# One-hot matmuls in place of a trip through DRAM for the first chunk's attention in a fused transformer block

## The chip, the cores and the metric

The kernel runs on one core of a Trainium2 chip. The metric is device time in microseconds (us) of one execution; lower is better. The five engines are named as the profile names them: PE (TensorE, the matrix engine, with its weight loads shown as PEld), DVE (VectorE), ACT (ScalarE), POOL (GpSimd) and SP (SyncE, which here only issues transfers). Each engine works through its own instructions in order, and waits at an instruction until what it needs is there.

## The reference

One block over 2048 rows of width 576, all in bfloat16: a layer norm shifted and scaled by vectors made from `c`, a local dilated attention, a second such layer norm, and a gated bilinear feed-forward layer of width 4608. Cut to what matters:

```python
W, dil = (8, 2)                     # H = 32 heads of Dh = 18
idx = pos[:, None] - (jnp.arange(W) * dil)[None, :]      # row s looks at rows s, s-2, ..., s-14
kg, vg = k[idx], v[idx]             # gathered per row and window step; idx < 0 is masked
attn = softmax(where(idx >= 0, einsum('bhsd,bhswd->bhsw', q, kg) * Dh**-0.5, -1e9))
o = einsum('bhsw,bhswd->bhsd', attn, vg)

sa, ca, ga, sb, cb, gb = split(silu(c) @ w_mod, 6)
x = x + ga * (attention(layernorm(x) * (1 + ca) + sa) @ wo)
h = layernorm(x) * (1 + cb) + sb
x = x + gb * (((h @ w_gate) * (h @ w_up)) @ w_down)
```

## The kernel before

**Tiling.** The 2048 rows are eight chunks of 256 rows (`CH`), each two halves j of 128 rows. Width 576 is four tiles of 128 and one of 64. The feed-forward layer works on groups of chunks (`GROUPS`: chunk 0 alone, then 1 and 2, 3 and 4, 5 and 6, then 7 alone): `gate_up` runs over 36 tiles of the 4608 columns, `down` over the same 36 tiles as contraction. While a group's feed-forward matmuls run, the attention of later chunks is worked off in small pieces between them; `spread` hands the pieces out by written costs. So from the first `gate_up` on, PE has matmuls nearly all the time.

**The setup stage.** Before the first `gate_up` can begin, chunk 0 must be through its attention, output projection and second layer norm, and chunks 1 and 2 through their Q, K and V projections. This stage is written out by hand, one call after another; the order of the calls is the order of the instructions on each engine. Its parts, by name:

- `load_wm`, `load_k`, `load_x`, `load_wgr`, `load_wgu` issue loads on SP, in one queue. A weight of 576 rows takes two transfers (512 rows and 64 rows). `wmA`, `wmB` and `wmC` hold blocks of `w_mod`.
- `mod_columns` makes the shift and scale columns from `wmA` or `wmB` (50 matmuls of one column); `mod_row` makes the row `ga` from `wmC`.
- `a_ln`, `a_norm` (layer norm statistics and normalisation, on DVE, the root on ACT), `a_t` (transposes on PE, evicted by ACT and DVE with shift and scale), `a_q` and `a_qj` (Q and K projections, evicted by ACT), `a_v` (V projection; its rows are evicted by ACT to `v_sb` and then written to the DRAM tensor `vd` by a POOL transfer).
- `b_ld` reads `vd` back, on POOL's queue: eight overlapping copies of 128 rows, each two rows further, into one tile `vsh` (1152 KB). So row p of the tile holds the eight value rows that query p looks at.
- `pj` (products of Q and shifted K on DVE), `lj` (sums per head by matmuls with the 0/1 matrix `ind`), `max_j` and `sum_j` (softmax on DVE, the exponential on ACT): the attention weights `attn0` of chunk 0, by query.
- `av_half` multiplies half of `vsh` by the weights on DVE (`b_mul`, 128x2304) and sums over the window with 20 matmuls by `ident` into `po`; ACT evicts to `oT`. `b_wj` is the output projection, `x1_half` the residual sum with the second norm's statistics, `transposed` the transposes into `h2T`, which `gate_up` reads.

**What sets the order around the loads.** Explicit dependencies made by `behind` hold back some transfers: the first load of `wo` waits until the first `vsh` has landed, and all loads behind it in SP's queue (the rest of `wo`, `wmC`, the residual rows) wait with it; the load of `wgr` waits for the second `vsh`; chunk 1's two `vsh` loads wait for the first two blocks `wgu`.

**The end.** `down` of the last group sums over 32 of the 36 tiles for both halves in turn, then finishes the 64-wide rests (`accr`), then the four last tiles of each half; DVE multiplies each half by `gb` (128x512), adds the residual to both halves, and SP stores each half's 128 x 576 rows.

Few lines say this best:

```python
    a_v(0, 0)                       # V, then Q and K, then the values come back through DRAM
    for g in range(3):
        a_qj(0, g, nc.scalar.copy)
    vsh_in = [b_ld(0, 0)]
...
        if dd4 == 0:
            behind(m, vsh_in[0])    # m: the first load of wo
```

Of the kernel before, what the change touches and what calls it, by code (L numbers as in the profile page):

```python
# [18 lines left out]
P = 128  # L19
# [24 lines left out]
def kernel(  # L44
# [55 lines left out]
    maskneg = consts.tile([P, W, H], BF, name="maskneg")  # L100
# [5 lines left out]
    wqk = wts.tile([P, KT, 2 * D], BF, name="wqk")  # L106
# [53 lines left out]
    def load_k(dst, wsrc, c0, n):  # L160
        r = nc.sync.dma_start(dst(slice(0, P), slice(0, KF)), wsrc[0:KF * P, c0:c0 + n].rearrange("(k p) n -> p k n", p=P))
        nc.sync.dma_start(dst(slice(0, 64), KF), wsrc[KF * P:D, c0:c0 + n])
        return r

    def load_wm(wm, bi, blk):
        return load_k(lambda p, k: wm[p, k, bi, :], w_mod, blk * D, D)
# [28 lines left out]
    zrow = sp.tile([HALO, D], BF, name="zrow")  # L195
    nc.gpsimd.memset(zrow[:], 0.0)
    nc.gpsimd.dma_start(vd[0:HALO, :], zrow[:])
    nc.gpsimd.memset(wqk[64:, KF, :], 0.0)
    for k in range(2):
# [6 lines left out]
                            pattern=[[-P, KT], [DH, H]], channel_multiplier=-1)  # L206
    nc.gpsimd.memset(maskneg[:], 0.0)
# [4 lines left out]
    for o_sb in o_sbs:  # L212
        nc.gpsimd.memset(o_sb[:, :, D:], 0.0)


    def ln_parts(src, tag):
# [15 lines left out]
        def norm(j):  # L232
            for d0, s0, n in ((0, 0, D), (D, D - 64, 64)):
                nc.vector.tensor_scalar(xn[:, j, d0:d0 + n], src(j)[:, s0:s0 + n], mv[:, j, 0:1], rstd[:, j:j + 1],
                                        ALU.subtract, ALU.mult)
        return xn, stat, rsq, norm

    def layernorm(src, tag):
# [4 lines left out]
        def norms():  # L243
            for j in range(ST):
                norm(j)
# [63 lines left out]
    def a_ln(i):  # L309
        x = x_in.pop(i)  # L310
        xn, rsq, norm = layernorm(lambda j: x[:, j, :], "a")
        aa[i] = dict(xn=xn, rsq=rsq, norm=norm)
# [54 lines left out]
    def a_v(i, j):  # L367
# [7 lines left out]
        v_sb = vstage.tile([P, DH, H], BF, name="v_sb")  # L375
# [3 lines left out]
        nc.gpsimd.dma_start(vd[r0:r0 + P, :], v_sb[:].rearrange("p d h -> p (d h)"))  # L379
# [78 lines left out]
    def av_half(j, hf, acc={}):  # L458
        b = bb[0]
        b_mul(0, j, 4 * hf, 4)  # L460
# [3 lines left out]
        v = b["vsh"][j][:].rearrange("p w d h -> p w (d h)")  # L464
        for w in range(4 * hf, 4 * hf + 4):
            for m in range(KT):
                d, m0 = (po[:, m, :], m * P) if m < KF else (po4[:], D - P)
                nc.tensor.matmul(d, lhsT=v[:, w, m0:m0 + P], rhs=ident[:], start=(w == 0 and m in (0, KF)),
                                 stop=(w == W - 1), skip_group_check=True)
# [167 lines left out]
    def down(gi, hh, bg):  # L637
        grp = GROUPS[gi]
        nj = ST * len(grp)
        last = FT - FB  # L640
        at = spread([(1.0, p) for p in bg], last)
        acc = [ps([P, 512], F32, "acc") for _ in range(nj)]
        accr = ps([P, 2 * ST, 64], F32, "accr")

        def mm_a(f, j):
            wb = wd_blk[gi * NBLK + f // FB]
            nc.tensor.matmul(acc[j][:], lhsT=hh[:, f, js(j)], rhs=wb[:, f % FB, 0:512],  # L647
                             start=(f == 0), stop=(f == FT - 1))
# [18 lines left out]
        for j in range(nj):  # L667
            for f in range(last, FT):
# [4 lines left out]
                                gb_bc[:, None, 512:D].to_broadcast([P, nj, 64]), ALU.mult)  # L673
        for j in range(nj):
            for f in range(last, FT):
                mm_a(f, j)
            nc.vector.tensor_tensor(o_ts[j][:, 0:512], acc[j][:], gb_bc[:, 0:512], ALU.mult)
# [33 lines left out]
    hT0 = aa[0]["hT"]  # L711
    nc.gpsimd.tensor_copy(sc_bc[:], sc[:, :, None].to_broadcast([P, KT, P]))
# [4 lines left out]
    a_ln(1)  # L717
    a_v(0, 0)
    for g in range(3):
        a_qj(0, g, nc.scalar.copy)  # L720
    vsh_in = [b_ld(0, 0)]
# [4 lines left out]
    def pj(j, w):  # L726
        off = HALO - DIL * (W - 1 - w) + j * P
        prods[j, w] = prodp.tile([P, KT, P], BF, name="prodj", tag="prod")
        nc.vector.tensor_tensor(prods[j, w][:], aa[0]["qT"][:, :, js(j)], aa[0]["kT"][:, :, off:off + P], ALU.mult)
# [18 lines left out]
    bb[0]["attn"] = attn0  # L748
# [11 lines left out]
    load_wm(wmB, 0, 3)  # L760
    load_wm(wmB, 1, 4)
    for dd4 in range(4):
        nk = (DH - dd4 + 3) // 4
        wsrc = bass.AP(A_wo.tensor, A_wo.offset + dd4 * D, [[DH * D, H], [4 * D, nk], [1, D]])
        m = nc.sync.dma_start(wo[dd4 * H:(dd4 + 1) * H, 0:nk, :], wsrc)
        if dd4 == 0:
            behind(m, vsh_in[0])
    load_wm(wmC, 0, 2)
    load_res(0)

    for w in range(2):
        pj(0, w)
    a_norm(1)
    for w in range(2, 4):
        pj(0, w)
    a_v(0, 1)
    vsh_in.append(b_ld(0, 1))
    for g in range(3):
        a_qj(1, g, nc.scalar.copy)
    for w in range(4):  # L780
        lj(0, w)
        pj(0, w + 4)
    a_t(1, False)
    for w in range(4, 8):
        lj(0, w)
    for w in range(2):
        pj(1, w)
    max_j(0)
    for w in range(2, 4):
        pj(1, w)  # L790
    a_q(1, 0)
# [3 lines left out]
    for w in range(4, 6):  # L795
        pj(1, w)
    sum_j(0)
    for w in range(6, 8):
        pj(1, w)
    a_q(1, 1)  # L800
    for w in range(4, 8):
        lj(1, w)
    max_j(1)
    a_q(1, 2)
    a_q(1, 3)
    av_half(0, 0)
    sum_j(1)
    a_q(1, 4)
    av_half(0, 1)
    a_v(1, 0)  # L810
    a_v(1, 1)
    mod_row(lambda p, k: wmC[p, k, 0, :], ga_bc)
    av_half(1, 0)
    x1_half = b_wj(0)
    a_ln(2)
    aa[2]["rsq"]()
    av_half(1, 1)
    aa[2]["norm"]()
# [110 lines left out]
```

## Time and profile before

| | us |
|---|---|
| median of 3 runs (lowest, highest) | 574.32 (572.67, 574.69) |
| the profiled execution, its time | 576.45 |
| its span, first to last instruction | 574.4 |
| its setup stage, until the first `gate_up` matmul (L595) starts | 62.36 |
| PE busy in the span | 548.4 |

The span is what the profile's views show; the profiled execution's own time is 2.05 us longer, and 2.13 us above the median of the runs. Matmuls of a stage overlap one another, so a row "x20, 1.29" of PE is 20 matmuls started one after another in about 1.1 us, with the last one's way through the array behind it. A number in square brackets at a timeline row is the idle time of that engine before it, with what ended it. In a list of waits the columns are total us, how many, and the longest. The chain of work that ended last is followed back from the last instruction, so its rows are what set the time.

### The profile page before, as it was taken

How to read it: one execution, taken by the hardware profiler on the slowest of the kernel's cores; microseconds unless marked ns; L12 is line 12 of the kernel's file. 1: busy time of each engine (PE TensorE's matmuls, PEld its weight loads, DVE VectorE, ACT ScalarE, POOL GpSimd, SP SyncE). 2: the span in 40 equal slices, each digit the busy share in tenths (PEclk: the TensorE clock that was granted, in tenths of full speed). 3: DMA queues.
4: the chain of work that ended last, by engine and by line, in shares of the span. 5: the costliest groups of instructions: out<-in, count | busy, mean ns of one | idle time of the engine just before them, and what ended most of it. 6: DMA issues, size and time to landing. Idle time of an engine off the chain costs nothing.

```text
span 574.4 us, 14284 instructions
## 1 busy us (share of the span) xinstructions
PE 548.4 (95%) x6024; PEld 320.3 (56%) x6058; DVE 323.7 (56%) x743; ACT 236.8 (41%) x546; POOL 66.0 (11%) x101
## 2 busy tenths in 40 slices
PE   3969998999999999999999999999999999999996
PEld 2846787666544444556444444555444444558863
DVE  5657679697568767613559759331647521324211
ACT  2533564434355555133145555113255552006630
POOL 5110201121300000111300000111200101110010
PEclk9997999999999999999999999999999999999999
DMA  8779999658756943648855924549854775468820
GB/s 248 241 220 279 354 299 328 194 156 264 247 179 217 289 126 69 123 133 191 292 194 184 296 96 120 106 114 280 296 167 138 231 213 184 124 188 241 283 72 34
DMA packets 90415, 115.05 MB, mean 200 GB/s; under 512 B 22288, under 2 KB 79712, under 8 KB 90224
## 3 DMA queue, kind: packets, MB, share of 16 engines
q1 hardware_dynamic: 77936, 65.69, 39.9%
q0 software_dynamic: 11808, 48.46, 26.4%
q8 instruction: 47, 0.77, 0.6%
q14 instruction: 16, 0.13, 0.1%
q10 hardware_dynamic: 608, 0.00, 0.1%
HBM read 105.14 MB, written 4.74 MB: 191 GB/s over the span
## 4 chain that ended last, share of the span: by engine, by line
PE 85%; DVE 6%; DMA 6%; ACT 1%; issue 1%; SPq 1%; DVEq 0%; ACTq 0%; POOLq 0%
PE pg L595 25%; PE pu L595 20%; PE acc L647 20%; PE pq L349 5%; PE accr L652 4%; PE lg L403 3%; PE pv L372 3%; PE pw L498 2%; DMA wmC<-in_w_mod_dram 2%; DMA vsh<-vd 1%; DMA wv<-in_A_wqkv_dram 1%; DMA vd<-v_sb 1%; DVE vsh L431 1%; DVE hh L624 1%; PE pa L298 1%
## 5 line engine op out<-in xcount | busy, mean ns | idle before, releaser
L595 PE MATMUL pg<-h2T,wgu 64*128 64x512 bf16 (+1 forms) x1440 | 276.1, 333 | 0.0
L595 PE MATMUL pu<-h2T,wgu 64*128 64x512 bf16 (+1 forms) x1440 | 272.4, 333 | 0.9 <-DMA wgu<-in_B_w_up_dram 0.9
L595 PEld LDWEIGHTS <-wgu 64*128 64x128 bf16 x2880 | 143.6, 94 | 107.6 <-DMA wgu<-in_B_w_up_dram 1.3
L619 ACT CAST u_sb<-pu 128x512 bf16<-128x512 f32 (+1 forms) x180 | 90.2, 501 | 160.9 <-PE pg L595 147.1
L647 PE MATMUL acc<-wd,hh 128*128 128x512 bf16 x516 | 135.1, 380 | 0.1
L624 DVE TENSOR_TENSOR hh<-g_sb,u_sb 128x512 bf16<-128x512 bf16 (+1 forms) x180 | 66.5, 370 | 106.0 <-ACT g_sb L620 101.4
L652 PE MATMUL accr<-wd,hh 128*128 128x64 bf16 x544 | 94.5, 193 | 1.4
L647 PEld LDWEIGHTS <-hh 128*128 128x128 bf16 x576 | 56.0, 98 | 64.2 <-issue 1.7
L620 ACT CAST g_sb<-pg 128x512 bf16<-128x512 f32 (+1 forms) x180 | 91.2, 506 | 0.1
L158 POOL DMA_DIRECT2D wd<-in_B_w_down_dram x41 | 31.0, 757 | 290.5 <-PE accr L652 247.4
L595 PE MATMUL pu<-h2T,wgr 64*128 64x512 bf16 (+1 forms) x180 | 60.3, 335 | 0.6 <-DVE dd L412 0.6
L595 PE MATMUL pg<-h2T,wgr 64*128 64x512 bf16 (+1 forms) x180 | 60.3, 335 | 0.0
L652 PEld LDWEIGHTS <-hh 128*128 128x128 bf16 x576 | 52.4, 98 | 2.2
L431 DVE TENSOR_TENSOR vsh<-vsh,attn 128x1152 bf16<-128x1152 bf16 (+1 forms) x60 | 45.8, 790 | 5.3 <-DMA vsh<-vd 5.3
L349 PE MATMUL pq<-hT,wqk 128*128 128x256 bf16 (+1 forms) x405 | 45.9, 262 | 1.0 <-ACT hT L252 0.4
L393 DVE TENSOR_TENSOR prod<-qT,kT 128x1280 bf16<-128x1280 bf16 x56 | 44.4, 819 | 0.0
L349 PEld LDWEIGHTS <-wqk 128*128 128x128 bf16 x405 | 34.4, 99 | 8.0 <-issue 1.9
L595 PEld LDWEIGHTS <-wgr 64*128 64x128 bf16 x360 | 21.1, 94 | 14.6 <-issue 1.3
L387 POOL DMA_DIRECT2D vsh<-vd x16 | 14.3, 895 | 113.8 <-DVE o_sb L442 68.2
L352 ACT CAST qT<-pq 128x512 bf16<-128x512 f32 x16 | 9.3, 584 | 42.9 <-PE pq L349 42.9
L672 DVE TENSOR_TENSOR t_r<-accr,gb_bc 128x256 bf16<-128x256 f32 (+1 forms) x5 | 1.9, 372 | 39.4 <-PE accr L652 39.4
L403 PEld LDWEIGHTS <-prod 128*128 128x128 bf16 x560 | 16.0, 96 | 12.0 <-DVE prod L393 6.3
(131 smaller groups left out, 435.2 us busy)
## 6 DMA issues: line engine op xcount, KB each, us to landing
wd<-in_B_w_down_dram POOLq DMA_DIRECT2D x41, 576.0 KB, 4.8
wgu<-in_B_w_gate_dram SPq DMA_DIRECT2D x45, 512.0 KB, 4.5
wgu<-in_B_w_up_dram SPq DMA_DIRECT2D x45, 512.0 KB, 6.0
vsh<-vd POOLq DMA_DIRECT2D x16, 1152.0 KB, 9.1
vd<-v_sb POOLq DMA_DIRECT2D x16, 144.0 KB, 5.1
x_r<-in_A_x_dram SPq DMA_DIRECT2D x8, 288.0 KB, 9.7
out_dram<-o_t SPq DMA_DIRECT2D x16, 144.0 KB, 7.0
vsh<-in_B_w_down_dram POOLq DMA_DIRECT2D x4, 576.0 KB, 5.1
```

The source lines that it names most:

```text
L158: return nc.gpsimd.dma_start(wb[:], B_w_down[r0:r0 + FB * P, :].rearrange("(k p) n -> p k n", p=P))
L349: nc.tensor.matmul(pq[:, gi, :], lhsT=wqk[:, kt, m * P:(m + 1) * P], rhs=hT[:, kt, cols], start=(kt == 0), stop=(kt == KT - 1))
L372: nc.tensor.matmul(pv[:], lhsT=hT[:, kt, js(j)], rhs=wv[:, kt, 0:VA * DH], start=(kt == 0), stop=(kt == KT - 1))
L393: nc.vector.tensor_tensor(prod[:], aa[i]["qT"][:], aa[i]["kT"][:, :, off:off + CH], ALU.mult)
L403: nc.tensor.matmul(b["lg"][:, j, w, :], lhsT=prod[:, m, js(j)], rhs=ind[:, m, :], start=(m == 0), stop=(m == KT - 1))
L431: nc.vector.tensor_tensor(v, v, at, ALU.mult)
L595: return nc.tensor.matmul(bank[:, 0:N], lhsT=lhs, rhs=rhs, start=first, stop=last, skip_group_check=True)
L619: nc.scalar.copy(u[:, 0:N], pu[:, 0:N])
L620: nc.scalar.copy(g[:, 0:N], pg[:, 0:N])
L624: nc.vector.tensor_tensor(hh[:, f, 0:N], gu[0][:, 0:N], gu[1][:, 0:N], ALU.mult)
L647: nc.tensor.matmul(acc[j][:], lhsT=hh[:, f, js(j)], rhs=wb[:, f % FB, 0:512], start=(f == 0), stop=(f == FT - 1))
L652: nc.tensor.matmul(accr[:, j, :], lhsT=hh[:, f, js(j)], rhs=wb[:, f % FB, 512:D], start=(f == 0 and j == 0), stop=(f == FT - 1), skip_grou ...
```

## The change

It touches the setup stage's chunk 0 and the last group's end.

1. **Values stay, weights move.** Chunk 0's V rows are kept in SBUF (`v0`), by key; of them only the last 16 rows are written to `vd`, for chunk 1. The attention weights, which are by query, are shifted to the keys: `shift_attn` runs 8 matmuls of 32 columns per half with slices of the one-hot matrix `shf`, and ACT copies the result to `at_k`. `av_mul` multiplies the V rows by these weights (DVE, 128x2304, both operands broadcast), and `av_sum` moves the products back to the queries while it sums: its 20 matmuls per quarter use slices of `shf` where `ident` stood. For the second half the 16 rows above it are made apart: `halo_values` (two matmuls), `halo_attn` (8 matmuls), one DVE product and 5 more matmuls in `av_sum`. The one-hot matrices are made on POOL: four memsets and twelve selects. The two `vsh` loads of chunk 0, the writes of its other 240 rows to `vd`, and the zero rows of `vd` go.
2. **Loads in one row.** `wmA` and `wmB` come as blocks of 1152 columns in one transfer each (and one for the last 64 rows). `wqk` is loaded as Q (576) and K (576) in place of three pieces; POOL copies K's last 64 columns next to Q's last 64.
3. **Order.** Q and K are loaded and projected ahead of V; the eight products of a half stand together; the layer norms of chunks 1 and 2 are normalised on ACT (four activations of 576 and 64 columns) and not on DVE.
4. **No holding back.** The loads of `wo`, `wgr` and chunk 1's `vsh` no longer wait for others by `behind`.
5. **The end.** In the last group the last eight tiles are left to the end in place of four; the second half's 512 columns are summed as two banks of 256, each multiplied, added and stored as soon as it is done; the 64-wide rests are done first.

The diff, cut to its core:

```diff
-    load_wm(wmA, 0, 0)
-    load_wm(wmA, 1, 1)
+    load_wm(wmA, 0)
+    load_k(lambda p, k: wqk[p, k, 0:D], A_wqkv, 0, D)
+    load_k(lambda p, k: wqk[p, k, DP:DP + D], A_wqkv, D, D)
     load_x(1)
     load_k(lambda p, k: wv[p, k, :], A_wqkv, 2 * D, D)
-    load_k(lambda p, k: wqk[p, k, 0:D], A_wqkv, 0, D)
-    load_k(lambda p, k: wqk[p, k, D:DP], A_wqkv, 2 * D - 64, 64)
-    load_k(lambda p, k: wqk[p, k, DP:2 * D], A_wqkv, D, D - 64)
...
+    shf = sp.tile([P, P + 2 * HALO], BF, name="shf")
+    p_q = sp.tile([P, (W - 1) * HALO + P], BF, name="p_q")
+    p_v = sp.tile([P, W, HALO], BF, name="p_v")
+    p_o = sp.tile([P, HALO], BF, name="p_o")
+    for t in (shf, p_q, p_v, p_o):
+        nc.gpsimd.memset(t[:], 0.0)
+    ones_at(shf[:], HALO, [[-1, P + 2 * HALO]], 1)
...
+    for w in range(W):
+        ones_at(p_o[:], -HALO * w, [[-1, HALO]], 1)
...
+        def norm_act():
+            nm = sp.tile([P, ST], F32, name="ln_nm", tag="ln_nm", bufs=2)
+            nc.vector.scalar_tensor_tensor(nm[:], mv[:, :, 0], -1.0, rstd[:], op0=ALU.mult, op1=ALU.mult)
+            for j in range(ST):
+                for d0, s0, n in ((0, 0, D), (D, D - 64, 64)):
+                    nc.scalar.activation(xn[:, j, d0:d0 + n], src(j)[:, s0:s0 + n], ACTF.Identity, bias=nm[:, j:j + 1],
+                                         scale=rstd[:, j:j + 1])
...
+        p0 = 0 if i else P - HALO if j else P
+        if p0 < P:
+            nc.gpsimd.dma_start(vd[r0 + p0:r0 + P, :], v_sb[p0:P].rearrange("p d h -> p (d h)"))
...
+    def shift_attn(j, attn, at_k):
+        r = ps([P, W, H], F32, "rot")
+        for w in range(W):
+            d = HALO + DIL * (W - 1 - w)
+            nc.tensor.matmul(r[:, w, :], lhsT=shf[:, d:d + P], rhs=attn[:, j, w, :], start=(w == 0), stop=(w == W - 1),
+                             skip_group_check=True)
+        nc.scalar.copy(at_k[:], r[:])
...
+    def av_mul(j, hf, v, at_k):
...
+        nc.vector.tensor_tensor(b["vsh"][j][:, ws], v[:, None, :, :].to_broadcast([P, 4, DH, H]),
+                                at_k[:, ws, None, :].to_broadcast([P, 4, DH, H]), ALU.mult)
...
+    nc.gpsimd.tensor_copy(wqk[:, :, D:DP], wqk[:, :, 2 * D:2 * D + 64])
...
-        if dd4 == 0:
-            behind(m, vsh_in[0])
...
+    for g in range(3):
+        a_qj(0, g, nc.scalar.copy)
+    a_ln(1)
+    for w in range(W):
         pj(0, w)
+    aa[1]["rsq"]()
     for g in range(3):
         a_qj(1, g, nc.scalar.copy)
+    aa[1]["norm"]()
+    v0[0] = a_v(0, 0)
+    for w in range(W):
+        lj(0, w)
+    max_j(0)
+    v0[1] = a_v(0, 1)
+    a_t(1, False)
     for w in range(4):
         pj(1, w)
     mod_columns(wmB, 1)
     for w in range(4):
         lj(1, w)
+    sum_j(0)
+    for w in range(4, W):
         pj(1, w)
+    a_q(1, 0)
+    shift_attn(0, attn0, at_k[0])
+    hv = halo_values(v0[0])
+    for w in range(4, W):
+        lj(1, w)
+    av_mul(0, 0, v0[0], at_k[0])
     a_q(1, 1)
     max_j(1)
     a_q(1, 2)
+    av_mul(0, 1, v0[0], at_k[0])
     a_q(1, 3)
+    av_sum(0, 0)
     sum_j(1)
     a_q(1, 4)
+    av_sum(0, 1)
+    shift_attn(1, attn0, at_k[1])
+    ha = halo_attn(attn0)
     a_ln(2)
     aa[2]["rsq"]()
+    a_v(1, 0)
+    av_mul(1, 0, v0[1], at_k[1])
+    mod_row(lambda p, k: wmC[p, k, 0, :], ga_bc)
     aa[2]["norm"]()
+    x1_half = b_wj(0)
...
+    av_mul(1, 1, v0[1], at_k[1])
+    av_sum(1, 0, hv)
...
+    a_v(1, 1)
...
+    av_sum(1, 1)
     a_t(2, False)
     x1_half = b_wj(1)
     load_x(3)
-    behind(load_wgr(), vsh_in[1])
+    load_wgr()
...
-    behind(b_ld(1, 0), wgu_in[0])
-    behind(b_ld(1, 1), wgu_in[1])
+    b_ld(1, 0)
+    b_ld(1, 1)
...
-        last = FT - FB
+        last = FT - (2 * FB if gi == NG - 1 else FB)
+        halves = [((0, 512),)] * (nj - 1) + [((0, 256), (256, 512)) if gi == NG - 1 else ((0, 512),)]
...
+                for h, (c0, c1) in enumerate(halves[j]):
+                    for f in range(last, FT):
+                        mm_a(f, j, (h,))
+                    cs = slice(c0, c1)
+                    nc.vector.tensor_tensor(o_ts[j][:, cs], acc[j][h][:], gb_bc[:, cs], ALU.mult)
+                    nc.vector.tensor_tensor(o_ts[j][:, cs], o_ts[j][:, cs], xs[j][:, cs], ALU.add)
+                    c1 = D if c1 == 512 else c1
+                    nc.sync.dma_start(out_flat[r0:r0 + P, c0:c1], o_ts[j][:, c0:c1])
```

More of the change, by code (lines that the diff above doesn't have):

```diff
@@ L463, in av_half, with add @@
         po, po4 = acc[j]
[L464 removed]
+        v = bb[0]["vsh"][j][:].rearrange("p w d h -> p w (d h)")
+        def add(src, m, c, first, last, rhs):
+            d, m0 = (po[:, m, c], m * P) if m < KF else (po4[:, c], D - P)
+            nc.tensor.matmul(d, lhsT=src[:, m0:m0 + P], rhs=rhs, start=first, stop=last, skip_group_check=True)
         for w in range(4 * hf, 4 * hf + 4):
+            d = HALO - DIL * (W - 1 - w)
             for m in range(KT):
[L467 to L469 removed]
+                add(v[:, w], m, slice(0, P), w == 0 and m in (0, KF), w == W - 1, shf[:, d:d + P])
+            if w == 0 and halo is not None:
+                for m in range(KT):
+                    add(halo[:].rearrange("p d h -> p (d h)"), m, slice(0, HALO), False, False, p_o[:])
         if hf == 1:
@@ L759 @@
     load_x(2)
-    load_wm(wmB, 0, 3)
-    load_wm(wmB, 1, 4)
+    load_wm(wmB, 3)
     for dd4 in range(4):
```

135 lines of the change are left out of this document (70 added, 65 removed).

## The prediction

> **What bounds the kernel now.** I read the chain first, cut to the setup stage (start, length, what).
>
> ```profile
> 4.67 7.80 DMA wv<-in_A_wqkv_dram
> 12.51 2.27 PE pv L372 x5
> ...
> 15.81 6.21 DMA vd<-v_sb
> ...
> 22.58 8.61 DMA vsh<-vd
> ...
> 33.03 10.16 DMA wmC<-in_w_mod_dram
> ...
> 43.33 0.59 PE pa L298
> ...
> 46.22 2.25 PE po L468 x20
> ```
>
> Up to 43.3 us the chain is transfers: V is loaded, projected, written to DRAM and read back, and only then does SP go on to `wo` and `wmC`. The waits of SP, PE and DVE in this stage say who pays:
>
> ```profile
> SPq L765 <- DMA vsh<-vd: 14.8, 1, 14.8
> ```
> ```profile
> PE pa L298 <- DMA wmC<-in_w_mod_dram: 3.5, 1, 3.5
> ```
> ```profile
> 41.28 1.36 DVE L431 TENSOR_TENSOR vsh<-vsh,attn 128x2304 bf16<-128x2304 bf16 x1 [5.28 <-DMA vsh<-vd]
> ```
>
> SP stood 14.8 us, so `wmC` came late and PE stood 3.5 us; DVE stood 5.3 us for the second `vsh`. The stages (us, each engine's busy time and count, PEclk, DMA share, GB/s) show what the PE gap costs beyond itself:
>
> ```profile
> 22.00:32.00 10.00, 8.31 (x174) 7.33 (x172) 8.90 (x24) 3.54 (x7) 1.57 (x3) 1.00 0.42 136
> ```
> ```profile
> 40.00:43.30 3.30, 0.00 (x0) 0.01 (x1) 2.02 (x3) 0.37 (x2) 0.55 (x2) 0.95 1.15 313
> 43.30:49.70 6.40, 6.16 (x35) 3.90 (x37) 3.58 (x10) 1.10 (x4) 0.00 (x0) 0.50 1.01 236
> 62.40:107.00 44.60, 42.00 (x809) 35.30 (x808) 33.28 (x72) 23.98 (x74) 5.40 (x8) 1.00 0.96 315
> ```
>
> The DMA engines are 42% busy while SP is held (22 to 32 us). After the gap PE gets a clock of 0.50 for 6.4 us, so about 3.2 us are lost on top of 3.5. From 62.4 us PE is busy 42.0 of 44.6 us, and so on to the end: what the setup stage gains is kept unless a load falls behind. The end itself is a chain on DVE:
>
> ```profile
> 568.25 1.74 PE acc L647 x8
> ...
> 570.02 0.69 DVE o_t L677
> 570.71 0.33 DVE o_t L680
> ...
> 571.14 0.34 DVE o_t L680
> ```
>
> **The change: front.** I follow the new order engine by engine and sum to the start of the first `gate_up` matmul, now 62.36. `wmA`: its second half let PE go at 9.54; one transfer of the same bytes ahead of everything else but x, I take 9.3 (8.5 if longer rows help, 10.3 if PE must wait for the tail). Behind it, 10 to 16 us moved 299 GB/s and 15 to 20 us 323: 0.66 MB each 2.1 us, so Q 11.4, K 13.5, x of chunk 1 14.4, V 16.4, `wmB` 21.5, `wo` 23.6, `wmC` 26; all 1 us earlier to 3 us later at the ends. 50 `mod_columns` matmuls at 0.92/25: 1.8, to 11.1; columns and first evictions, 10.50 to 12.1 before: 1.6, to 12.7. Before, PE was at half rate from 12.5 to about 15.9 (a 504-column matmul 0.41 us, later 0.21), so Q and K of half 0 start at 0.104 us each: 25 take 2.6, to 15.3; the last 20 are half at the slow rate, 1.6, to 16.9. K's 64 copied columns: POOL's added memsets and selects are 4 of 0.2 to 0.3, 4 of 0.29 to 0.47 and 8 of 16 columns, under the 0.29 of 128 columns, at most 5.4 us in all; the zero rows that go took 1.5. POOL had reached 8.2, so it is free by 12.1 and the copy (half the 0.72 of `sc_bc`) ends at 13.5+0.45=14.0, before PE wants it at 14.8: nothing, covered by the Q matmuls; 1 us if the copy took twice as long and K were 0.5 late. ACT evicts K (0.59, and 0.2 behind PE) at 17.7; before, the first `pj` ran at 19.11.
>
> **Middle.** DVE: eight `pj` at 0.445 end at 21.3 (before 25.6, with other work between). PE meanwhile: 45 Q/K matmuls 2.7, `a_v` 1.23, the mask and 40 `lj` 1.33, to 22.2; then `a_v` 1.23, transposes 0.57, `mod_columns` 1.6, to 25.6. ACT's normalisation, 2 of 576 and 2 of 64 columns: the nearest rows are 0.59 (128x512) and 0.21 (128x64), so 1.7 us where DVE took 1.18; it ends at 23.3, just as PE comes to the transposes (23.4): nothing, but each 0.1 us more shows. From here DVE leads: `max_j` 0.85, evictions 0.7, four `pj` 1.8, columns 0.5, `sum_j` 1.4, to 28.5; four `pj`, to 30.3; then `av_mul` 1.35 by L431's row, `max_j` 0.85, `av_mul` 1.35, `sum_j` 1.4, to 35.3. PE waits some 2.1 us in all in this piece (1.9 before in 22 to 34 us), then runs through: `a_q` 2.7, `av_sum` 1.13, `a_q` 1.09, `av_sum` 1.13 to 36.6, where before the second half's `vsh` was still to come. New on PE: `shift_attn` twice and `halo_attn`, 24 matmuls at the 0.030 of `lj`, 0.75; `halo_values` 0.26; 5 halo matmuls 0.15: 1.2 us. On ACT: 0.37 twice, 0.8, 0.2; ACT is busy under half of this stage, and `at_k` of half 1 comes at 38.0, DVE's products at 39.4 and 41.4, PE wants them at 40.8 and 43.3.
>
> **Back.** `a_v` 1.23, `mod_row` 1.24 at full rate (2.9 before), `b_wj` 1.21, `av_sum` 1.28, `a_v` 1.23, `av_sum` 1.13, to 44.4; transposes 0.57; 0.6 for `oT`'s eviction; `b_wj` 1.21; Q and K of chunk 2, transposes and V as before: 55.0. These sums leave out small gaps: the same steps of before, from 50.2 to 62.4, took 12.15 us where my way of summing gives about 11.8, so I add 1.0 over the stage. 56.0, that is 6.4 us off; 8.2 at the good end, 3 at the bad. It agrees with what goes: gap and half rate 6.7, front 1.4, less 1.2 of new matmuls.
>
> Loads that I cost at nothing: `wgr` and three `wgu` (4.3 MB) follow x of chunk 3, whose buffer is free at 23.3; at 300 GB/s they land by about 44, 12 us ahead. Chunk 1's `vsh` loads now wait for its V rows only (`a_v` at 38 and 43): landed by 60, wanted some 18 us after the first `gate_up`, at 74. Behind them POOL's queue holds loads wanted at 100. If that cover goes, `gate_up` starts late one for one.
>
> **First group and end.** In the first `gate_up` PE waited 0.9 us for `wgu`, PEld 1.2; 2.3 MB of `vsh` now lie further ahead: 0.4 off (0 to 2.1). At the end, behind the last matmul, 0.69+0.33+0.44+0.10 become 128x256 steps: 0.43 (between 0.69 for 512 and 0.29 for 128) and 0.28 (between 0.42 and 0.18): 0.85 off; the last store has no other beside it, 0.2; 16 matmuls of 256 for 8 of 512 cost nothing (0.109 against 0.215). 1.0 off (0.6 to 1.4).
>
> Sum: 6.4+0.4+1.0 = 7.8. The profiled execution took 576.45 (span 574.4), 2.13 above the median 574.32; the median becomes 566.5.
>
> **A rule against it.** The row: PE's half rate lasted 3.4 us after 12.5 but 6.4 us after 43.3. The Trainium skill (TensorE: Matmul & The Clock Gate, Part 1) says that the activity window is free-running, so the release shifts with where the first matmul falls. By the rows I used 3.4; by the rule the front could get the 6.4 of the other start, 3 us more at half rate, 1.5 us: 568.0. The trace agrees that two starts can differ; I leave it inside the forecast's bounds.
>
> **The rivals.**
> - DVE's product at one element a cycle because now both operands are broadcast (before: one). 128x256 and 128x512 from PSUM take 0.42 and 0.69, 1.06 ns per element, so 2304 take 2.6 and not 1.35. Four of them on DVE's leading piece: 1.6 to 2.5 us on the path after the slack of 1.4 to 1.9. 568.8. Against it: L431's broadcast is at full pace already.
> - Loads late: one order in SP's queue, and everything behind Q and K moves with them. K at 17 and `wmB` at 24 give 3.2 us: 569.7. For it: loads of 64 KB and up took 7 to 10 us to land; against it: there is less to load.
> - The start is given back: the DMA engines were 0.96 busy from 62.4 to 107, so an earlier `gate_up` only waits for its weights. 573.3, the end's gain alone. Against it: PE waited only 2.1 us for them, and 2.6 MB less is moved.
> - Slower: PE's waits for DVE between 24 and 31 us bring the clock down as the gap at 40 did. Each us of matmul work at half rate costs one; half rate from 26 to about 47, some 18 us of matmul work at the full rate, less 7.8, gives 584. It decides from 7.8+2.9=10.7 us of such work. Against it: 22 to 32 us had PE 83% busy with waits of up to 1.4 and a clock of 1.00.
>
> **How the numbers follow.** About 0.5%, 2.9 us, is what a measurement of this kernel can tell from no change: faster is below 571.4. Chances: forecast 0.64, broadcast 0.10, late loads 0.14, given back 0.07, clock 0.05. The forecast's own bounds (3+0+0.6 to 8.2+2.1+1.4 off) are 562.6 to 570.7; taking in the broadcast and the late loads, 563 to 571 leaves out about 2 in 10. Faster: 0.64+0.10 and most of 0.14, 0.85; same 0.09; slower 0.06.
>
> **What would show it.** Right: the first L595 matmul near 56; no DVE wait for `vsh` and no PE wait over 2 us after 13 us; clock 1.00 from 17 us on; `wmC` landed before 30; the first 128x2304 product near 31 at 1.35 us; the last DVE step 0.75 us after the last matmul. Wrong: a mean near 2.6 at `av_mul`; PE waiting for `wqk`, `wmB` or `wgu`; a clock of 0.5 past 20 us; the first `gate_up` longer than the 44.7 us that it took.

## The result, and the profile after

The changed kernel takes 568.55 us (median of 5 runs, 567.49 to 570.20) where the kernel before takes 574.32 (5 runs, 572.67 to 574.79): 5.8 us less, a ratio of 0.9911 with a 95% interval of 0.9886 to 0.9937. Forecast were 566.5 and a range of 563 to 571. The sign and the range held; 2.0 of the 7.8 us did not come.

Every profile below is one execution. The changed kernel's has a span of 568.4 us (its own time is 570.20, 1.65 above the median; that of before was 2.13 above its own), against 574.4. The chain of work that ended last, in order of time, cut to the setup stage (start, length, what):

```profile
4.80 9.11 DMA wqk<-in_A_wqkv_dram
14.05 0.46 POOL wqk L801
14.55 5.38 PE pq L375 x70
...
30.43 4.73 PE pq L375 x25
...
35.15 1.12 PE po L534 x20
...
```

Where the chain of before ran through `vd` and `vsh`, this one runs through K's load, POOL's copy and then almost only PE. The longest waits by engine and line in 8 to 58 us (us in total, times, longest) say the same:

```profile
DVE vsh L523 <- ACT at_k L494: 2.9, 1, 2.9
POOL wqk L801 <- DMA wqk<-in_A_wqkv_dram: 2.8, 1, 2.8
...
PE pm L311 <- DMA wmA<-in_w_mod_dram: 1.1, 1, 1.1
...
PE pq L375 <- DVE hT L276: 1.0, 1, 1.0
```

No wait for `wmC` or for a `vsh` load is left, and PE's two waits of 1 us lie ahead of Q. DVE's wait of 2.9 us at half 1's `av_mul` holds nobody up. The new product takes 1.35 us, as the one of before did (1.36), and ACT's normalisation is longer than I took (2.29 for 1.7); first the instructions of the product's line (duration in ns, min/median/max), then two rows of the timeline (start, length):

```profile
L523 DVE TENSOR_TENSOR vsh<-v,at_k x4: 1349/1352/1358, 30.0 to 41.5; 128x2304 bf16<-128x2304 bf16 x4
```
```profile
21.48 2.29 ACT L257 ACTIVATE ln_xn<-x_t,ln_nm,ln_rstda 128x576 bf16<-128x576 bf16 x4 [0.92 <-DVE ln_nm L254]
...
29.97 1.35 DVE L523 TENSOR_TENSOR vsh<-v,at_k 128x2304 bf16<-128x2304 bf16 x1
```

The stages (us, each engine's busy time and count in the order PE, PEld, DVE, ACT, POOL; then PEclk, DMA share, GB/s):

```profile
22.00:27.50 5.50, 5.28 (x109) 4.23 (x106) 4.09 (x12) 4.62 (x12) 0.66 (x1) 1.00 1.10 267
27.50:34.40 6.90, 6.49 (x55) 4.45 (x53) 6.70 (x13) 3.29 (x9) 0.00 (x0) 0.51 1.03 214
34.40:56.80 22.40, 22.11 (x254) 17.30 (x255) 15.53 (x40) 15.57 (x43) 3.25 (x5) 1.00 0.90 281
56.80:101.40 44.60, 42.02 (x809) 35.26 (x808) 33.26 (x72) 23.99 (x74) 5.39 (x8) 1.00 0.85 275
```

PE is busy 22.11 of 22.40 us up to the first `gate_up`, and that takes the same 44.6 us as before: nothing of the earlier start is given back there. But from 27.5 to 34.4 us the granted clock is 0.51 although PE waits for nothing long: the 25 `pq` matmuls of the chain take 4.73 us there, and 2.7 where the same step runs at full rate (50.28 us, 2.73). DVE's part of the end is as forecast; its last step ends 0.79 us behind the last matmul (1.60 before):

```profile
564.39 0.37 DVE o_t L758
564.76 0.02 issue
564.78 0.29 DVE o_t L759
```

Difference of the two spans, 6.0 us: the start of the first `gate_up` matmul 5.6 (62.36 to 56.77), from there to the last matmul 0.1, from that to the end of the span 0.3 (4.42 to 4.12).

### The profile page after: what moved, and what is told of

Read it like the earlier page. It is cut to its first block, busy times and chain, and to the rows that moved or that the text cites. A ratio compares the mean times of both kernels' runs of the same rounds, so it can differ in the third digit from the quotient of the medians.

```text
span 568.4 us, 14437 instructions
## 1 busy us (share of the span) xinstructions
PE 549.2 (97%) x6090; PEld 325.8 (57%) x6125; DVE 322.6 (57%) x740; ACT 242.0 (43%) x559; POOL 66.7 (12%) x113
## 4 chain that ended last, share of the span: by engine, by line
PE 89%; DVE 7%; DMA 2%; ACT 1%; issue 1%; SPq 1%; POOL 0%; ACTq 0%; POOLq 0%
PE pg L668 26%; PE pu L668 20%; PE acc L723 20%; PE pq L375 7%; PE accr L727 4%; PE pv L398 3%; PE lg L432 3%; PE pw L571 2%; DMA wqk<-in_A_wqkv_dram 2%; DVE vsh L460 1%; PE po L534 1%; DVE hh L697 1%; DVE prodj L816 1%; DVE prod L422 1%; DVE vsh L467 0%
## 5 line engine op out<-in xcount | busy, mean ns | idle before, releaser
L668 PEld LDWEIGHTS <-wgu 64*128 64x128 bf16 x2880 | 141.5, 94 | 107.4 <-DMA wgu<-in_B_w_up_dram 1.0
L723 PE MATMUL acc<-wd,hh 128*128 128x512 bf16 (+1 forms) x534 | 134.4, 372 | 0.2
L375 PE MATMUL pq<-hT,wqk 128*128 128x256 bf16 (+1 forms) x405 | 49.7, 279 | 1.8 <-DVE hT L276 1.3
L375 PEld LDWEIGHTS <-wqk 128*128 128x128 bf16 x405 | 37.5, 106 | 9.5 <-issue 1.3
L460 DVE TENSOR_TENSOR vsh<-vsh,attn 128x1152 bf16<-128x1152 bf16 x56 | 40.4, 751 | 0.0
L668 PEld LDWEIGHTS <-wgr 64*128 64x128 bf16 x360 | 19.0, 94 | 14.6 <-issue 1.3
L416 POOL DMA_DIRECT2D vsh<-vd x14 | 12.5, 892 | 84.9 <-DVE o_sb L471 68.8
```

The costliest lines, as they stand in the source:

```text
L375: nc.tensor.matmul(pq[:, gi, :], lhsT=wqk[:, kt, m * P:(m + 1) * P], rhs=hT[:, kt, cols], start=(kt == 0), stop=(kt == KT - 1))
L460: nc.vector.tensor_tensor(v, v, at, ALU.mult)
L668: return nc.tensor.matmul(bank[:, 0:N], lhsT=lhs, rhs=rhs, start=first, stop=last, skip_group_check=True)
L723: nc.tensor.matmul(a[:], lhsT=hh[:, f, js(j)], rhs=wb[:, f % FB, c0:c1], start=(f == 0), stop=(f == FT - 1))
```

## The experiments

Two questions were open. First, the clock of 0.51: it is the place of the rival that I had given 0.05, so does it fall because of what runs there, and what does it cost? Second, of what is the gain made: of the gap at 40 us and the clock behind it, as I summed it, of the order of the loads, of the end, or of the trip as such? My theory throughout was the sum in the prediction.

**Does work on PE between 22 and 27 us hold the clock?** Between 23.3 and 26.7 us PE runs transposes, 50 matmuls of one column and 20 of 32, with no wait over 0.34 us. Two kernels add matmuls whose result nobody uses behind `mod_columns(wmB, 1)`, with equal time and very different numbers of columns:

```diff
+    fill = ps([P, 512], F32, "fill")
+    for _ in range(6):
+        nc.tensor.matmul(fill[:], lhsT=ident[:], rhs=wv[:, 0, 0:512], start=True, stop=True)
```

> The changed kernel with six more matmuls of 512 columns on PE (their result is used by nobody) behind the second mod_columns, where the changed kernel's trace has 3.4 us of transposes, 1-column and 32-column matmuls in a row (23.3 to 26.7 us) before the clock falls to 0.50 (27.6 to 34.4 us). Theory A, the clock is granted by how many columns PE streams, so those 3.4 us look idle to it: the clock stays 1.00 to the first gate_up, which starts at 54.5 to 55.5 in place of 56.8; about 566.7 us, 1 to 2 us faster than the changed kernel though PE has 1.3 us more work. Theory B, the clock fell because of PE's short waits for DVE: the fall stays, gate_up starts 1 us later at 57.8, about 569.5 us.

The other has 42 matmuls of 32 columns (`fill[:, 0:32]`, `wv[:, 0, 0:32]`) in that place:

> The same place and nearly the same added PE time (42 matmuls of 32 columns at 0.030 us, 1.3 us), but few columns. Theory A (columns): the clock falls as in the changed kernel or earlier, gate_up starts at 57.5 to 58.5, about 569.5 to 570 us. Theory C, the clock is granted by the time in which PE has any matmul under way: it stays 1.00 as with the dense filler, gate_up at 55, about 566.7 us. Theory B (waits): falls too, 569.5 us.

Measured: 568.91 us (ratio 0.9929, 0.9907 to 0.9950) and 568.55 (0.9929, 0.9907 to 0.9951), no different from the change; the 1 to 2 us of theory A did not come. The stage of the clock's fall, in the profile of the first and then of the second:

```profile
27.50:34.40 6.90, 6.61 (x90) 5.64 (x88) 6.76 (x14) 3.86 (x10) 0.00 (x0) 1.00 1.04 209
```
```profile
27.50:34.40 6.90, 6.36 (x87) 5.38 (x86) 6.73 (x13) 3.95 (x10) 0.00 (x0) 1.00 1.03 207
```

Both held the clock, so columns alone are not what counts. In all the traces of this study that have the change's setup stage with K at its place and no filler there, six, the clock fell behind the thin stretch, for 3.4 us in five and 6.8 in one; in the two with a filler it did not. Over all runs the mean clock of the whole execution, in which falls at other places count too, was 0.999 or more in 6 of 12 with filler and in 3 of 17 runs of the change (plain, again, and with the old end). But the filler costs its own 1.2 to 1.3 us, and a fall of 3.4 us at half rate costs 1.7: it buys nothing that can be measured. What decides the fall, whether the spacing, the columns or the moment, is not settled.

**The end taken back.** The changed kernel with the last `down` as it was:

```diff
-        last = FT - (2 * FB if gi == NG - 1 else FB)
+        last = FT - FB
-        halves = [((0, 512),)] * (nj - 1) + [((0, 256), (256, 512)) if gi == NG - 1 else ((0, 512),)]
+        halves = [((0, 512),)] * nj
-        if gi == NG - 1:
+        if False:
```

> The changed kernel with the end of the kernel before (four tiles left, both halves as whole banks of 512, both residual sums behind the last matmul). By the prediction's term the end is worth 1.0 us: 569.5 us. By the two traces, in which last matmul to end of span is 4.4 us before and 4.1 after, it is worth 0.3: about 568.9 us; the span then ends about 2.8 us behind DVE's last step, where the changed kernel has 3.3.

569.60 us (ratio 0.9942, 0.9920 to 0.9963). The change itself was timed on another chip: by the medians this is 1.05 us above it, by the ratios 1.8, and the intervals overlap. Beside the kernel before, on one chip, what is left without the new end is 3.3 us (2.1 to 4.6). The same setup code had one fall of 3.4 us here, not two, and started the first `gate_up` at 54.80 instead of 56.77: the two windows of the first trace are not a constant of the kernel.

**The hold taken from SP's queue in the kernel before.** The trip stays; `wo` and `wmC` no longer wait for it:

```diff
         m = nc.sync.dma_start(wo[dd4 * H:(dd4 + 1) * H, 0:nk, :], wsrc)
-        if dd4 == 0:
-            behind(m, vsh_in[0])
```

> The kernel before without the one dependency that holds the loads of wo (and with it wmC and all behind it) until the first vsh has landed; everything else as before. Theory D, the trip through DRAM is the cost: wmC is there before PE wants it, but vsh now shares the DMA engines, DVE still waits 5 us or more for the second vsh and PE's clock still falls; 0 to 2.5 us faster than before, 572 to 574.3 us. Theory E, the held queue is the cost: PE's wait of 3.5 us and the half clock go, 5 us or more faster, 569.3 us or less.

574.77 us, 1.0031 of before (1.0005 to 1.0057): slightly slower, so theory E fell, and the 0 to 2.5 us that theory D allowed did not come either. PE no longer waits for `wmC`, the clock falls for 3.4 us from 49.9 instead of for 6.8 from 43, the first `gate_up` comes at 58.89, and yet nothing is gained over the runs. The chain of the setup (start, length, what):

```profile
22.54 10.22 DMA vd<-v_sb
...
33.04 5.97 DMA vsh<-vd
...
39.10 1.36 DVE vsh L431
...
49.43 3.60 PE pq L349 x18
```

The second `vsh` lands at 39.0; DVE's product, two layer norms and ACT's evictions hang on it, and PE comes to `a_q(2, 0)` behind them. The queue's wait was one way in which the trip was paid, not the only one.

**The end alone, on the kernel before** (its whole `down` is that of the change, nothing else is):

```diff
-        last = FT - FB
+        last = FT - (2 * FB if gi == NG - 1 else FB)
...
+        if gi == NG - 1:
+            for j in range(nj):
+                nc.vector.tensor_tensor(o_ts[j][:, 512:D], t_r[:, j, :], xs[j][:, 512:D], ALU.add)
...
```

> The kernel before with only the new end (the last down stage of the change, nothing else). Theory of the prediction: the end is worth 1.0 us, so the time is 1.0 us under the kernel before on this chip, ratio 0.9983; last DVE step 0.75 us behind the last matmul. Rival, from the two traces: last matmul to end of span went from 4.4 to 4.1 us only, since what follows the last DVE step grew from 2.8 to 3.3 us, so 0.3 us, ratio 0.9995. The kernel of the change with the old end gave 569.6 against 568.55 for the whole change, on two chips, which speaks for 1.0.

572.75 us against 574.14 beside it, ratio 0.9972 (0.9953 to 0.9990): 1.4 us by the medians, 0.6 to 2.7 by the interval. The 0.3 of the pair of traces is ruled out, barely. What the pair hid lies in what follows the last DVE step until the span ends. With the old end it is 2.8 us in the kernel before and 3.7 in the changed one; with the new end it is 2.5 here and 3.3 in the change. So the new end shortens the time from the last matmul to the end of the span by 1.1 us in either kernel (4.42 to 3.30, 5.27 to 4.12), and the rest of the change lengthens it by 0.8. The last store takes 1.6 us to land here and in the change; behind its landing the closing steps of the program take 0.9 us here and 1.7 in the change. Why they do was not tried.

This execution told more about the setup, which is word for word that of before. `wmC` was there in time, the clock stayed at 1.00, and still the first `gate_up` matmul came only at 58.23. Its stages where before had the gap and the half rate, and then its chain:

```profile
40.00:43.30 3.30, 3.12 (x36) 2.12 (x34) 3.13 (x8) 0.96 (x4) 0.55 (x1) 1.00 1.01 225
43.30:49.70 6.40, 4.16 (x48) 3.12 (x46) 6.16 (x18) 2.64 (x8) 0.00 (x0) 1.00 1.04 294
```
```profile
22.49 7.49 DMA vd<-v_sb
29.98 0.28 issue
30.26 9.75 DMA vsh<-vd
40.11 1.36 DVE vsh L431
...
48.91 1.49 ACT hT L252 x3
50.43 2.13 PE pq L349 x18
```

Gap and half rate are not in every execution of before. Where they are missing, DVE's chain behind the trip takes their place: from 43.3 to 49.7 us DVE is busy 6.16 of 6.40 and PE 4.16.

**The gap of before filled.** 14 matmuls with an unused result, where PE had stood for `wmC`:

```diff
     a_v(1, 1)
+    fill = ps([P, 512], F32, "fill")
+    for _ in range(14):
+        nc.tensor.matmul(fill[:], lhsT=ident[:], rhs=wv[:, 0, 0:512], start=True, stop=True)
     mod_row(lambda p, k: wmC[p, k, 0, :], ga_bc)
```

> The kernel before with 14 matmuls of 512 columns whose result nobody uses, put between a_v(1, 1) and mod_row, where PE stood 3.5 us for wmC. They fill the gap (14 by 0.22 = 3.0 us) and take nothing from any engine that is waited for. Theory of the prediction (the gap brings PE to a clock of 0.50 for 6.4 to 6.8 us, of which half is lost): the clock holds at 1.00 from 43 to 50 us, the first gate_up matmul starts near 59.1 instead of 62.4, and the time is 3.2 us under the kernel before, ratio 0.9944. Rival A: the clock falls all the same, now or a window later, by a rule that goes not by this gap alone: no gain, ratio 1.000. Rival B: the stage is bound by DVE's wait for the values and not by PE: the clock holds and the start moves by less than 1 us.

573.81 us against 574.14, ratio 1.0003 (0.9983 to 1.0024): no gain; the 3.2 us of my theory did not come, though the clock held as it said. In its profile the clock holds through the filler and behind it:

```profile
39.00:42.30 3.30, 3.30 (x21) 1.55 (x20) 2.73 (x6) 0.70 (x2) 1.00 (x2) 1.00 1.21 331
42.30:50.00 7.70, 7.30 (x81) 5.42 (x80) 6.78 (x19) 3.37 (x11) 0.00 (x0) 1.00 0.99 258
```

The first `gate_up` matmul comes at 58.40: 4.0 us before the 62.36 of the first trace, but level with the 58.23 of the kernel just told, which has neither gap nor filler. So a held clock is worth what I said against the execution that I priced from, and nothing against one that does not lose it.

**Warming PE ahead of Q.** In all traces so far the first `pq` matmuls are slow, at a listed clock of 1.00: they start 0.107 us apart, and later 0.056. Half microseconds in which this changes; the number in brackets counts the `pq` matmuls under way, some of which began just before; in the filler kernel with 512 columns and in that with 32, whose code is the same up to there:

```profile
15.00:15.50 0.50, 0.50 (x9) 1.00 1.10 316
15.50:16.00 0.50, 0.50 (x12) 1.00 1.07 263
```
```profile
17.50:18.00 0.50, 0.50 (x9) 1.00 1.10 406
18.00:18.50 0.50, 0.50 (x13) 1.00 1.05 392
```

The step to the fast spacing comes at 15.4 in one and at 17.8 in the other, and the projections end 1.05 us apart. The experiment:

```diff
+    warm = sp.tile([P, 512], BF, name="warm")
+    nc.vector.memset(warm[:], 0.0)
+    fill = ps([P, 512], F32, "fill")
+    def warm_up(n):
+        for _ in range(n):
+            nc.tensor.matmul(fill[:], lhsT=warm[:, 0:P], rhs=warm[:], start=True, stop=True)
+    warm_up(10)
...
+    warm_up(2)
     mod_columns(wmA, 0)
+    warm_up(3)
```

> The kernel of the change with 15 matmuls of 512 columns whose result nobody uses ahead of Q: 10 at the very start, 2 behind the first transposes, 3 behind mod_columns(wmA). In four traces of the same front PE's first matmuls of Q and K took 0.065 us each and more until 15.3, 16.8, 17.1 and 17.9 us and 0.038 behind that, at a listed clock of 1.00. Theory: PE needs some microseconds of work, counted from a point that differs between executions, before it runs at full rate; with work from 1.5 us on it is at full rate before Q begins. Then the 70 matmuls behind K's arrival take 4.2 us instead of 4.4 to 5.7, the first gate_up matmul starts 1.0 us earlier, and the time is 1.0 us under the change on the same chip, with less scatter. Rival: the slow rate is that of the loads of Q and K or of the first use of the weights: no change.

569.07 us (ratio 0.9905, 0.9883 to 0.9928), no different from the change on that chip. The warming worked and was lost again, as the granted clock of these stages shows:

```profile
6.00:11.60 5.60, 3.84 (x65) 2.37 (x64) 2.30 (x13) 0.94 (x4) 4.59 (x20) 1.00 1.07 292
11.60:15.00 3.40, 2.94 (x24) 2.37 (x24) 1.67 (x7) 1.44 (x4) 0.86 (x2) 0.52 1.09 320
```

PE was at full rate by 6.9 (two 512-column matmuls in 0.59 us, where ten took 4.06 at the start), and fell for exactly 3.4 us just as Q began; Q's first 20 matmuls took the same 2.58 us as without warming.

**The changed kernel again**, on that chip:

> The changed kernel again, on the chip of the other three, as their measure. Expected 0.991 of the kernel before; and the clock in its profiled execution between 24 and 36 us, which fell for two stretches of 3.4 us in one execution and for one in another with the same code: theory (the fall depends on where the chip's own window lies over the thin matmuls from 23.3 to 26.7 us): none, one or two such stretches. Rival (PE's waits decide): two, as in the first.

569.31 us, ratio 0.9913 (0.9891 to 0.9934): the gain repeats on a second chip. In the setup the clock fell once, from 25.6 to 29.0 us, and the first `gate_up` matmul came at 53.88; my theory would have allowed none, one or two, so this says little for it. The clock fell a second time in the first `gate_up`, from 87.1 to 90.5 us, and from the first `gate_up` matmul to the last matmul this execution took 509.4 us where the first took 507.5.

**V and x(1) loaded ahead of Q and K, in the changed kernel:**

```diff
     load_wm(wmA, 0)
-    load_k(lambda p, k: wqk[p, k, 0:D], A_wqkv, 0, D)
-    load_k(lambda p, k: wqk[p, k, DP:DP + D], A_wqkv, D, D)
     load_x(1)
     load_k(lambda p, k: wv[p, k, :], A_wqkv, 2 * D, D)
+    load_k(lambda p, k: wqk[p, k, 0:D], A_wqkv, 0, D)
+    load_k(lambda p, k: wqk[p, k, DP:DP + D], A_wqkv, D, D)
```

> The changed kernel with the loads of x(1) and V ahead of those of Q and K, the order that before had; nothing else is moved. Theory: the front is set by K's arrival. K comes 0.96 MB later, at some 300 GB/s 3.2 us, so POOL's copy ends near 17.6 instead of 14.5; PE is warm by then, and the 70 matmuls take 3.9 us instead of 4.4 to 5.7, so they end near 21.6 instead of 18.9 to 20.0. The first gate_up matmul is 1.6 to 2.7 us later and the time some 2 us above the changed kernel: about 0.995 of the kernel before instead of 0.991. Rival (PE has slack behind the projections, as DVE's products and not PE set the stage; or x being early makes up for it): no difference from 0.991.

571.63 us, ratio 0.9931 (0.9912 to 0.9950). By the ratios 1.1 us above the change, by the medians (on different chips) 2.3 to 3.1: near the 2 expected, though the two intervals overlap. PE's waits:

```profile
PE pq L375 <- DMA wqk<-in_A_wqkv_dram: 3.5, 1, 3.5
...
PE pq L375 <- POOL wqk L801: 0.8, 1, 0.8
```

K's matmuls began at 18.07, half a microsecond behind the forecast, but PE was not at full rate: the 70 took 6.09 us instead of 3.9, and the first `gate_up` came at 58.86, 2.1 us behind the change's first trace and 5.0 behind its second. So the slow start is not over at a fixed time of the kernel: with PE idle from 11.4 to 14.9 us the full rate came at 22.3.

**The order alone, in the kernel before** (Q and K ahead of x and V in the loads, and their projections of half 0 ahead of the first values; the trip stays):

```diff
-    load_x(1)
-    load_k(lambda p, k: wv[p, k, :], A_wqkv, 2 * D, D)
     load_k(lambda p, k: wqk[p, k, 0:D], A_wqkv, 0, D)
...
+    load_x(1)
+    load_k(lambda p, k: wv[p, k, :], A_wqkv, 2 * D, D)
...
-    a_ln(1)
-    a_v(0, 0)
     for g in range(3):
         a_qj(0, g, nc.scalar.copy)
+    a_ln(1)
+    a_v(0, 0)
```

> The kernel before, with one part of the change alone: Q and K loaded ahead of x(1) and V, and the projections of Q and K of half 0 ahead of the first values on PE; the values still go through DRAM. Theory: the trip through DRAM sets the stage, V arrives some 4 us later (16.4 instead of 12.5), so everything that waits for the shifted values is later by 2 to 4 us and the kernel 1.5 to 4 us slower than before, ratio 1.003 to 1.007: the order of the loads pays only once the trip is gone. Rival: the order itself is what gained, by PE starting on Q while V loads: faster than before by 1 us or more.

575.58 us against 575.01, ratio 1.0011 (0.9993 to 1.0029): neither what I expected nor a gain. V's first projection ran 4.3 us later (16.76 for 12.51), but the second half's, which the chain goes through, stayed where it was (18.17 for 18.29), and so did the first `gate_up` (58.63). It is the second half's trip that counts; the order has no value while it is there.

This trace tells something else: PE stood for `wmC` here too, and no half rate came behind it (a wait; then a stage):

```profile
PE pa L298 <- DMA wmC<-in_w_mod_dram: 2.6, 1, 2.6
```
```profile
43.30:49.70 6.40, 6.19 (x76) 5.05 (x77) 6.17 (x17) 2.83 (x9) 0.00 (x0) 1.00 1.00 235
```

With the gap and without the half rate the first `gate_up` starts 0.4 us behind the 58.23 of the kernel that has neither. So far as these single traces show it, the gap by itself is nearly free, and what made the first trace late is the half rate behind it.

**Chunk 1's normalisation back on DVE, in the changed kernel:**

```diff
-        xn, rsq, norm = layernorm(lambda j: x[:, j, :], "a", i < 3)
+        xn, rsq, norm = layernorm(lambda j: x[:, j, :], "a", i == 2)
```

> The changed kernel with the normalisation of chunk 1 on DVE, as before had it, instead of on ACT (chunk 2 stays on ACT). Theory: DVE's four steps (1.5 us for chunk 0's four) come between the products of half 0 and the maximum, and DVE, which PE waits for at 28 to 29 us (0.2 us per pair of products), is 0.7 to 1.5 us later there; so is PE: 0.7 to 1.5 us slower than the changed kernel. Rival: DVE stood idle for 1.5 us there (it waited for K's columns from 16.6 to 18.1), ACT was the tighter one, with 2.29 us for the four steps ahead of the values' eviction: same or up to 0.5 us faster.

568.02 us, ratio 0.9879 (0.9856 to 0.9901). My theory fell: nothing is slower. DVE does in 1.19 us what took ACT 2.29, in time in which it had stood idle:

```profile
20.49 1.19 DVE L250 TENSOR_SCALAR ln_xn<-x_t,ln_mva,ln_rstda 128x576 bf16<-128x576 bf16 x4
```

By the ratios it would even be 1.9 us faster than the change, but the two never ran side by side, and the first `gate_up` starts at 53.82, as it does in the change's second trace (53.88). I take it as the same; its median is the lowest of all versions.

**The last logits of chunk 2 moved out of the first `gate_up`**, where PE waits for DVE's products in every trace:

```diff
+    log2 = B_log(2)
     gbg = {0: B_log(1) + B_av(1) + [res(2), (0.0, load_wm5), (0.0, lambda: load_wd(0))] + log2[:11],
...
+    dbg = {0: [gb_row] + [p for _, p in log2[11:]] + first + out_qkv0(2, 4) + [lambda: [b_ld(3, j) for j in range(ST)]],
```

> The changed kernel with the last logits and the softmax of chunk 2 moved from the end of the first gate_up to the start of the first down stage. In every trace PE waits for the last products of chunk 2 on DVE at 84 to 97 us, 1.3 to 2.3 us in all, before and after the change. Theory: these waits go, 1.0 to 1.8 us under the changed kernel, ratio about 0.988. Rival: DVE is behind there by as much work as it has, and the first down stage, where DVE is busy 38 of 50 us, takes the wait over: no change.

570.17 us, ratio 0.9909 (0.9885 to 0.9933): no gain, as the rival said. The wait for the products has gone from 1.7 us in the change's second trace (first fence) to 0.3, and comes back in the `down` stage as a wait for DVE's layer norm (second fence, this kernel):

```profile
PE lg L432 <- DVE prod L422: 1.7, 2, 1.2
```
```profile
PE tr_pA L287 <- DVE ln_xn L250: 1.7, 2, 1.4
```

## Why the prediction was right, and where it fell short

Stretches from 22 us to the first `gate_up` matmul in six traces; "waits" is the stretch less PE's busy time, "clock" the stretch times one minus the granted clock:

| execution | first `gate_up` | stretch | waits | clock |
|---|---|---|---|---|
| before, first trace | 62.36 | 40.36 | 6.8 | 3.2 |
| before's setup with the new end | 58.23 | 36.23 | 5.3 | 0 |
| before's setup with the order of Q, K and V alone | 58.63 | 36.63 | 6.0 | 0 |
| the change, first trace | 56.77 | 34.77 | 0.9 | 3.5 |
| the change, second trace | 53.88 | 31.88 | 0.5 | 1.6 |
| the change with 512-column filler | 53.90 | 31.90 | 0.5 | 0 |

- **The mechanism held.** What went are PE's waits behind the trip, 4.4 to 6.4 us of them, whichever executions are compared; about 1.2 us of new matmuls came. Neither the released queue nor the order of the loads gains anything while the trip is there, which the two kernels with one of these alone show; and the change keeps most of its gain with V loaded first (0.9931), with the old end (0.9942) and with chunk 1's normalisation on DVE (0.9879). No kernel has the trip alone removed, and the loads in one row were not tried alone, so the trip is shown to be the cause by elimination only.
- **The front held, in part by luck.** K landed at 13.9 (13.5 forecast), the copy was done at 14.5 (14.0), PE began on K at 14.55 (14.8), the projections of both halves ended at 19.9 (19.6). But two errors cancel in the last figure: PE began on Q at 11.64 and not at 12.7, and came to full rate at 17.4 and not at 15.9. POOL's copy cost 0.34 us rather than nothing. ACT's normalisation took 2.29 for 1.7, and that cost nothing either: undoing it changed nothing in the setup.
- **The start at 56.0 was met by luck.** It was measured at 56.77, but 3.5 us of that are the clock's, which the sum did not have; without them it would be near 53.3, an estimate from the table. The change's five other traces with K at its place and no filler behind `mod_columns` start between 53.39 and 54.80. So my steps were 2 us or more too long: PE was to wait 2.1 us for DVE in the middle, and from 22 us to the first `gate_up` it waited 0.5 to 0.9 in all, with the small gaps for which I had added 1.0.
- **The step that failed is "gap and half rate 6.7".** I took both from one execution, 2.13 us above the median, and set the whole against the median; my check (6.7 + 1.4 - 1.2 = 6.9) rested on it, and so did the 62.36 from which the 6.4 was taken. Another execution of the same setup code has neither and starts its `gate_up` 4.1 us earlier, since behind the gap stood a second limit: DVE's chain from the second `vsh`. With the gap alone (2.6 us, clock 1.00) the start is at 58.63, so, as far as single traces show it, nearly all of the 4 us are the half rate's. Against the execution that has neither, the start gains 4.4 us (58.23 to 53.88), not 6.4. Even these do not all reach the end: in that pair of traces the spans differ by 1.7 us only, since the second trace of the change lost 1.8 to the clock's fall at 87 us and 0.8 in the closing steps. The runs are the better measure: 3.3 us (2.1 to 4.6) without the new end and 1.4 (0.6 to 2.7) for the new end alone, each beside before on its own chip. How often the gap and the fall come in a run without a profile is not known.
- **The clock of the change was not 1.00 from 17 us on.** I had it as a rival with 0.05, for PE's waits between 24 and 31 us. The place was right and the cause not: there was no wait over 0.34 us. Its price was 1.7 us in most traces and 3.4 in the first, since a fall lasted one or two stretches of 3.4 us, where I had it last until 47 us. It doesn't turn the sign, since before has falls of its own: of 17 of its runs beside the first experiments the four with a mean clock of 0.998 or more took 570.70 to 571.75, the other thirteen 572.67 to 576.84.
- **The first group gave at most the 0.1 of the first pair, not 0.4.** PE's wait for `wgu` is still 0.8 us (0.9 before); fewer `vsh` loads ahead of it did not help.
- **The end** was 1.0 by the sum. Its own part held: 1.1 us in the traces, 1.4 beside before, 1.05 by medians from two chips. What the sum put at nothing are the 0.8 us by which the rest of the change lengthens the closing steps.
- **The other rivals fell.** The broadcast product takes 1.35 us and not 2.6. The loads came in time; the kernel with K 3.5 us later shows what it would have cost. The first `gate_up` took 44.6 us in the first trace, as before, so the start was not given back to the loads there.
- **The rule against it.** Seven traces of one front went to full rate between 14.8 and 17.8 us, where I had taken 15.9 from before: 3.0 us of scatter, and the projections of both halves end between 18.4 and 19.9 us. By the Trainium skill (TensorE: Matmul & The Clock Gate, Part 1) the activity window is free-running and the release moves with where it lies; the traces agree. From Q's first matmul on the half rate lasted 3.3 to 6.1 us, 5.7 in the first trace: nearly the 6.4 that I had bounded it with. The same part lets the clock fall after an idle window; here it fell with PE 5.28 of 5.50 us busy just before, so by this trace's measure of busy the rule is too narrow.

## What to carry to other kernels

A stall seen in one trace is worth, in the median, only what the next limit behind it leaves: here a 3.5 us gap with a slow clock behind it hid a DVE chain that lets the next stage start 4.1 us earlier at best, and filling the gap or freeing the queue gained nothing. If the profiled execution is slower than the median, the excess may be in the very stall that is to be removed; price against a second execution of the same code, or take the excess off the stall. When a forecast time is met, look whether its terms were: here a start came out right because a lost clock made up for steps that were priced too long. And find the transfer that the whole chain goes through: while it is there, the order of loads, a released queue or a held clock gained nothing; once it was gone, the order was worth some 1 us by the ratios, though the intervals overlap.

## What was not expected of the hardware

- The granted clock falls for 3.4 us, or twice that, with PE 96% busy, behind some 3 us of matmuls of few columns (1, 32) and transposes; matmuls of 512 or of 32 columns put there both kept it up. It came in six of six traces without filler, for 3.4 us in five and 6.8 in one. In four of the fourteen traces it also fell later, between 75 and 110 us, for 3.4 or 6.8 us.
- A slow start isn't listed as a lower granted clock: `pq` matmuls began 0.107 us apart at a clock of 1.00 until 14.8 to 17.8 us, then 0.056.
- Warming PE early is not kept: with 15 matmuls of 512 columns before 11.5 us the clock went down to 0.52 from 11.6 to 15.0 us, and the first 20 matmuls of Q took 2.58 us as they do cold.
- Executions of one setup code differ by 3.5 us in when a transfer behind a DRAM round trip lets PE go on (wanted at 39.8: there in one, at 43.3 in another).
- An idle gap on PE of 3.5 us had a clock of 0.50 behind it, one of 2.6 us at the same place in another kernel had not.
